# Gated MLP stage on one core: values normalised on ACT behind the next tile's gelu, transposes and last spatial products one output tile later, the last stores on two queues

## The chip, the core and the metric

The kernel runs on one core of a Trainium2 chip. The metric is the device time of one execution in microseconds (us). A core has five engines with an instruction queue each, and each works through its own queue in order: PE (matmul; PEld is its weight load), DVE (vector), ACT (activation), POOL (the general engine) and SP (which here issues DMAs). They meet only through semaphores: an instruction waits until those that write its inputs, or that still read the buffer it will overwrite, have signalled.

## The reference, cut to what matters

Three layers follow one another: attention with a learned position bias, an MLP with a layer norm, and a gated MLP. The change lies in the gated MLP, the last 230 us or so. With x of shape 4 x 576 x 512 and d_ff of 1024:

```python
h = x @ w_in
h = 0.5 * h * (1.0 + np.tanh(c * (h + 0.044715 * h ** 3)))     # gelu
u, v = (h[..., :d_ff // 2], h[..., d_ff // 2:])
mu = np.mean(v, axis=-1, keepdims=True)
var = np.mean((v - mu) ** 2, axis=-1, keepdims=True)
v_n = (v - mu) / np.sqrt(var + 1e-06) * g_ln
v_s = np.einsum('ts,bsd->btd', w_sg, v_n) + b_sg[None, :, None]
gated = u * v_s
return (x + gated @ w_out).astype(np.float32)
```

## The kernel before

Every product runs as three matmul products of split operands (a high and a low part: high by high, high by low, low by high), so each result that feeds a product is split by two instructions: the high part is copied out on ACT (`split_hi`, L110), the low part is the difference, on POOL or DVE (`split_lo`, L113).

The gated MLP is a list of groups, `seq`, worked off by `step`. There are five kinds, for batch element b:

- `g_T` ("transpose"): four PE transposes of a 128-row tile of x into one of two PSUM tiles `pt` (L490), copied out and split into `x2h` (ACT) and `x2l` (DVE).
- `g_v` ("value tile"): 12 matmuls into `psa` (L117), gelu, then layer norm without its gain, then the split into `blk` (or into `vre` and `vro` for the tile that holds the 64 leftover rows of two batch elements).
- `g_u` ("u tile"): 24 matmuls of 288 columns into `psa` (L1210), gelu.
- `g_s` ("spatial product"): 28 matmuls of 288 columns (L1228) with the values as weights, multiplied by u on DVE (L1237, L1238), split.
- `g_o` ("output tile"): 12 matmuls (L117), the residual added on DVE (L1260), stored by DMA.

`psa` has three buffers, so a group's matmuls wait until the group three places before has been read out of PSUM for the last time; for a value or u tile that last read is L1154, the end of its gelu. `pt` has two buffers, so a transpose waits for the `x2l` of the second transpose before it. The SBUF tile `v`, of which there are three, holds a value tile until its low part is taken, and an output tile until it is stored.

The gelu is four instructions in turn: Square on ACT (L1148), L1149 on DVE, Tanh on ACT (L1153), L1154 on DVE. `gelu` returns them as two functions, `first` (Square, L1149) and `second` (Tanh, L1154). For a value tile `second` goes on with the row statistics on DVE (L466, L467). What is left of a group is put off to the next steps: `step` first issues the group's matmuls, then goes through three places (z = 0, 1, 2), issuing in each what earlier groups left for that place and then the group's own function. A value tile leaves for the next step the inverse root of the variance on POOL (`scale`, L470 and L471; L473 and L474 too where the subtraction is folded into a bias) in place 0, the normalisation itself (`apply`, in place, of tile `v`) in place 1 and the copy of the high part in place 2, and for the step after that the low part on POOL in place 0.

`seq` interleaves the groups by `mix`, which takes one of each list in turn. Value tiles come in four batches, 5, 4, 5 and 4 of them, with four u tiles behind the first batch, output tiles of the element before and transposes of the element after mixed behind the second and third, and two output tiles, an `idle` step and the spatial products behind the last. Below, "batch b" means the value tiles of element b and what follows them. Output tiles are stored by SP; the tile j = 4 holds leftover rows of two elements and is stored as two halves.

Of the kernel before, what the change touches and what calls it, by code (L numbers as in the profile page):

```python
# [93 lines left out]
def block_kernel(  # L94
# [6 lines left out]
    act, dve, pool, pe, sp = nc.scalar, nc.vector, nc.gpsimd, nc.tensor, nc.sync  # L101

    def new_pool(name, bufs, stack=None, **kw):
        return (stack or ctx).enter_context(tc.tile_pool(name=name, bufs=bufs, reuse_waits="tile", **kw))
# [4 lines left out]
    def split_hi(o, i, **kw):  # L109
        act.activation(o, i, AF.Copy, **kw)  # L110

    def split_lo(o, i, hi, eng=None):
        (eng or dve).tensor_tensor(out=o, in0=i, in1=hi.bitcast(F32), op=ALU.subtract)  # L113

    def product(ps, terms, start=True, stop=True):
        for j, (w, x) in enumerate(terms):
            pe.matmul(ps, lhsT=w, rhs=x, start=start and j == 0, stop=stop and j == len(terms) - 1)  # L117
# [148 lines left out]
    with ExitStack() as c:  # L266
# [21 lines left out]
        for f in (load_q, load_k):  # L288
# [9 lines left out]
            out=W.rearrange("p (g h) -> p g h", h=8), in0=w8.unsqueeze(1).to_broadcast([128, 4, 8]), in1=ind.unsqueeze(2).to_broadcast([128, 4, 8]), op=ALU.mult,  # L298
# [157 lines left out]
    def block_pair(p):  # L456
        return [p.tile([128, 4, 512], F32R, name="blk") for _ in range(2)]

    def norm_parts(sm, src, eps, dst, eng):

        s6 = sm.tile([128, 6], F32, name="s6")
        mv = sm.tile([128, 2], F32, name="mv")
        rs = sm.tile([128, 2], F32, name="rs")

        def stats():
            dve.bn_stats(out=s6, in_=src)  # L466
            dve.bn_aggr(out=mv, in_=s6)  # L467

        def scale():
            pool.tensor_scalar(out=mv[:, 1:2], in0=mv[:, 1:2], scalar1=eps, scalar2=1.0, op0=ALU.add, op1=ALU.mult)  # L470
            pool.tensor_tensor(out=rs[:, 0:1], in0=mv[:, 1:2], in1=mhalf, op=ALU.pow)  # L471
            if eng is not dve:
                pool.tensor_scalar(out=mv[:, 0:1], in0=mv[:, 0:1], scalar1=-1.0, scalar2=0.0, op0=ALU.mult, op1=ALU.add)  # L473
                pool.tensor_tensor(out=rs[:, 1:2], in0=mv[:, 0:1], in1=rs[:, 0:1], op=ALU.mult)  # L474

        def apply():
            if eng is act:
                act.activation(dst, src, AF.Identity, scale=rs[:, 0:1], bias=rs[:, 1:2])
            elif eng is pool:
                pool.tensor_scalar(out=dst, in0=src, scalar1=rs[:, 0:1], scalar2=rs[:, 1:2], op0=ALU.mult, op1=ALU.add)  # L480
            else:
                dve.tensor_scalar(out=dst, in0=src, scalar1=mv[:, 0:1], scalar2=rs[:, 0:1], op0=ALU.subtract, op1=ALU.mult)  # L482

        return stats, scale, apply
# [37 lines left out]
    def ln_T(blk, j):  # L522
        p = transpose4(xn[blk][j][0])
        th, tl = xT[blk]
        o = slice(128 * j, 128 * j + 128)
        split_hi(th[:, :, o], p)
        split_lo(tl[:, :, o], p, th[:, :, o])
# [112 lines left out]
    with ExitStack() as c:  # L640
        smp = new_pool("asm", 1, c)
        sm = smp.tile([128, 48], F32, name="sm")
# [228 lines left out]
        for u in range(-1, NU):  # L871
            for w in SEQ:
                du, name, *args = w.split()
                v, args = u + int(du), list(map(int, args))
# [54 lines left out]
    def T_groups(b):  # L929
        return [g_T(b, j) for j in ([4] if b % 2 == 0 else []) + [0, 1, 2, 3]]  # L930
# [4 lines left out]
    with ExitStack() as c:  # L935
# [125 lines left out]
        for blk in range(5):  # L1061
# [9 lines left out]
            T = [lambda j=j: ln_T(blk + 1, j) for j in range(len(tiles[blk + 1]))] if blk < 4 else []  # L1071
# [63 lines left out]
    sm = new_pool("qsm", 4)  # L1135
# [7 lines left out]
    def gelu(T, dst, cols):  # L1143


        def first():
            q = T["s"] = tp.tile([128, S], F32, name="sq")[:, :cols[0] * cols[1]].rearrange("p (a b) -> p a b", a=cols[0])
            act.activation(q, T["p"], AF.Square, scale=GELU_SQ)  # L1148
            dve.scalar_tensor_tensor(out=q, in0=q, scalar=GELU_C, in1=T["p"], op0=ALU.add, op1=ALU.mult)  # L1149

        def second():
            q = T["s"]
            act.activation(q, q, AF.Tanh)  # L1153
            dve.scalar_tensor_tensor(out=dst(), in0=q, scalar=1.0, in1=T["p"], op0=ALU.add, op1=ALU.mult)  # L1154

        return first, second

    def g_v(b, j):
        T = {}

        def pe_():
            xh, xl = x2R[b // 2] if j == 4 else [t[:, :, 128 * j:128 * j + 128] for t in x2T[b]]
            T["p"] = psA.tile([128, 2, 512], F32, name="psa")[:, :1]
            product(T["p"][:, 0], [(x[:, k], w[:, k]) for x, w in ((xh, vh), (xh, vl), (xl, vh)) for k in range(4)])
            if j == 0:
                vn[b] = block_pair(wb)
            if j == 4:
                vr[b // 2] = [vp.tile([128, 512], F32R, name="vre"), vp.tile([128, 512], F32R, name="vro")]

        def dst():  # L1170
            T["v"] = tv.tile([128, 512], F32, name="v")
            return T["v"].unsqueeze(1)

        first, second_ = gelu(T, dst, (1, 512))

        def second():
            second_()
            T["n"] = norm_parts(sm, T["v"], 4e-6, T["v"], dve)
            T["n"][0]()

        def parts():

            if j < 4:
                return [(slice(0, 128), vn[b][0][:, j], vn[b][1][:, j])]
            e, o = vr[b // 2]
            return [(slice(0, 64), e[:64], e[64:]), (slice(64, 128), o[64:], o[:64])]

        def post():
            for r, hi, _ in parts():
                split_hi(hi, T["v"][r])  # L1190

        def late_():
            for r, hi, lo in parts():
                split_lo(lo, T["v"][r], hi, pool)

        return pe_, first, second, [(lambda: T["n"][1](), lambda: T["n"][2](), post), (late_, None, None)]

    def g_u(b, m):
# [51 lines left out]
    def g_o(b, j):  # L1250
        T = {}

        def pe_():
            gh, gl = gr[b // 2] if j == 4 else [t[:, :, 128 * j:128 * j + 128] for t in gT[b]]
            T["p"] = psA.tile([128, 2, 512], F32, name="psa")[:, 0]
            product(T["p"], [(x[:, k], w[:, k]) for x, w in ((gh, oh), (gh, ol), (gl, oh)) for k in range(4)])

        def first():
            o = tv.tile([128, 512], F32, name="v")
            dve.tensor_tensor(out=o, in0=T["p"], in1=x_sb[:, 4 * b + j if j < 4 else 16 + b // 2], op=ALU.add)  # L1260
            if j < 4:
                sp.dma_start(out=out[b, 128 * j:128 * j + 128], in_=o)
            else:
                for q in range(2):
                    sp.dma_start(out=out[b - 1 + q, 512:], in_=o[64 * q:64 * q + 64])

        return pe_, first, None, []

# [2 lines left out]
    def step(g):  # L1271
        pe_, first, second, later = g
        now = [q.pop(0) for q in live][::-1]
        pe_()
        for z, own in ((0, first), (1, second), (2, None)):
            for f in now:
                if f[z]:
                    f[z]()
            if own:
                own()  # L1280
        live[:] = [q for q in live if q]
        if later:
            live.append(list(later))

    def idle():
        return (lambda: None), None, None, []

    def v_groups(b):
        return [g_v(b, j) for j in ([4] if b % 2 == 0 else []) + [0, 1, 2, 3]]

    def mix(*lists):

        return [g for n in range(max(map(len, lists))) for x in lists for g in x[n:n + 1]]

    s = {b: [g_s(b, d) for d in range(4)] for b in range(B)}
    u = {b: [g_u(b, d) for d in range(4)] for b in range(B)}
    o = {b: [g_o(b, j) for j in range(4)] + ([g_o(b, 4)] if b % 2 else []) for b in range(B)}
    t = {b: T_groups(b) for b in range(1, B)}
    seq = v_groups(0) + u[0] + mix(s[0][:3], t[1]) + [s[0][3]] + u[1]
    seq += [t[2][0]] + v_groups(1) + mix(o[0], t[2][1:]) + mix(s[1], u[2])  # L1300
    seq += v_groups(2) + mix(o[1], t[3]) + mix(s[2], u[3])
    seq += v_groups(3) + o[2][:2] + [idle()] + s[3] + o[2][2:] + o[3]
    seq += [idle() for _ in range(4)]
    for n, g in enumerate(seq):
        mark(f"gmlp {n}")
        step(g)
# [54 lines left out]
def build(tc, nc, aps, out):  # L1361
    a = {n: (p.bitcast(I32) if n in ("moe_w_ch1", "moe_w_ch2", "moe2_w_in", "moe2_w_out") else p) for n, p in aps.items()}
    with tc.manual_schedule():
        block_kernel(tc, nc, a, out)
# [18 lines left out]
```

## Time and profile before

| | |
|---|---|
| runs | 982.79, 987.43, 988.38 us; median 987.43 us |
| profiled execution | 982.66 us, its span in the trace 980.7 us |
| granted TensorE clock | 0.993 of full speed on average |
| PE, DVE, ACT, POOL busy | 96%, 77%, 50%, 46% of the span |

All rows below are of the one profiled execution; its times count from the start of the span. The end of a matmul is modelled in the trace, so a stretch without PE work is best read from the starts of matmuls. "x12" behind a row means that twelve instructions in a row were merged; "[0.59 <-DVE v L1154]" means that the engine stood idle for 0.59 us before it, until that instruction released it.

### The profile page before, as it was taken

To read this page: it belongs to the slowest core of one execution; us is meant where nothing else is said; L and a number is where in the kernel's file an instruction comes from. 1 tells how busy PE (TensorE), PEld (TensorE's weight loads), DVE (VectorE), ACT (ScalarE), POOL (GpSimd) and SP (SyncE) were. 2 spreads that over 40 slices of the span, in tenths; PEclk is the share of its full clock that TensorE was granted. 3 is DMA by queue.
4 is the path that set the end of the run, shared out by engine and by line. 5 is a ranking of instruction groups with operands and counts; after the bars stand their busy time and mean duration, and the time that the engine had idled before them with its cause. 6 is when DMAs were issued, how large, how long until landed. Compare 5 with 4: busy or idle time off the path is not lost. (4 is left out here: it accounts for less than half of the span.)

```text
span 980.7 us, 16000 instructions
## 1 busy us (share of the span) xinstructions
PE 937.7 (96%) x5729; PEld 813.9 (83%) x5729; DVE 754.9 (77%) x1460; ACT 485.7 (50%) x1090; POOL 450.9 (46%) x556
## 2 busy tenths in 40 slices
PE   7879999999898999999999999999999999998998
PEld 2269998989898878888888888888888897988986
DVE  8989888899887858886769797979765847475462
ACT  8969987989797854322222222323132434242320
POOL 0086997989899744332314334333300423132241
PEclk9999999999999999999999999999999999999999
DMA  7875445436443271113022333332213000001002
GB/s 245 280 265 187 160 153 181 152 124 199 140 143 121 67 257 68 44 31 106 21 99 93 119 95 119 95 118 91 101 65 121 1 2 22 22 1 54 1 23 75
DMA packets 53007, 104.49 MB, mean 107 GB/s; under 512 B 9152, under 2 KB 20160, under 8 KB 52672
## 3 DMA queue, kind: packets, MB, share of 16 engines
q1 hardware_dynamic: 52096, 103.02, 31.3%
q8 instruction: 45, 0.74, 0.3%
q10 hardware_dynamic: 832, 0.46, 0.2%
q14 instruction: 34, 0.28, 0.1%
HBM read 75.08 MB, written 28.38 MB: 105 GB/s over the span
## 5 line engine op out<-in xcount | busy, mean ns | idle before, releaser
L170 POOL TENSOR_TENSOR cvl<-cvl,cvt 128x512 f32<-128x512 f32 x44 | 56.9, 1292 | 206.3 <-DVE cvt L167 186.8
L117 PE MATMUL psh<-blk,w1h 128*128 128x512 f32 (+1 forms) x640 | 151.4, 368 | 0.0
L636 ACT ACTIVATE hh<-psh 128x512 fp32r<-128x512 f32 (+1 forms) x80 | 43.9, 552 | 185.7 <-PE psh L117 177.7
L117 PEld LDWEIGHTS psh<-blk,w1h 128*128 128x128 f32 x640 | 113.5, 188 | 20.7 <-DVE hl L637 0.3
L689 DVE CUSTOM_DVE_ANT_0 ct<-s,bias 128x576 f32<-128x576 f32 x144 | 107.4, 753 | 24.6 <-PE s L683 15.0
L703 ACT ACTIVATE a<-ct,sm 128x576 f32<-128x576 f32 x144 | 112.2, 779 | 3.3 <-POOL v L107 2.3
L1031 DVE TENSOR_TENSOR x_sb<-psy,x_sb 128x512 f32<-128x512 f32 x144 | 97.3, 683 | 9.1 <-PE psy L117 8.6
L709 PE MATMUL pt<-ident,a 128*128 128x128 f32 x576 | 87.1, 279 | 13.8 <-DVE at0l L113 13.8
L637 DVE SCALAR_TENSOR_TENSOR hl<-psh,hh 128x512 fp32r<-128x512 f32 (+1 forms) x80 | 50.5, 633 | 56.0 <-ACT hh L636 55.9
L117 PE MATMUL psy<-w2h,hh 128*128 128x512 f32 x288 | 90.4, 395 | 0.1
L117 PE MATMUL psy<-w2l,hh 128*128 128x512 f32 x288 | 89.0, 390 | 0.0
L117 PE MATMUL psy<-w2h,hl 128*128 128x512 f32 x288 | 88.8, 390 | 0.0
L709 PEld LDWEIGHTS pt<-ident,a 128*128 128x128 f32 x576 | 70.6, 143 | 15.7 <-DVE at0l L113 15.4
L117 PE MATMUL psh<-blk,w1l 128*128 128x512 f32 (+1 forms) x320 | 79.0, 368 | 0.0
L683 PE MATMUL s<-kh,q 128*128 128x288 f32 x320 | 73.5, 320 | 2.7 <-DVE sm L689 0.9
L683 PE MATMUL s<-kl,q 128*128 128x288 f32 x320 | 66.5, 298 | 0.0
L117 PEld LDWEIGHTS psh<-blk,w1l 128*128 128x128 f32 x320 | 56.8, 189 | 10.0
L117 PEld LDWEIGHTS psy<-w2h,hl 128*128 128x128 f32 x288 | 54.1, 188 | 11.5
L117 PEld LDWEIGHTS psy<-w2l,hh 128*128 128x128 f32 x288 | 54.0, 188 | 11.4
L171 POOL TENSOR_TENSOR cvw<-cvl,cvw 128x512 f32<-128x512 f32 x44 | 59.9, 1362 | 3.5
L117 PEld LDWEIGHTS psy<-w2h,hh 128*128 128x128 f32 x288 | 52.4, 188 | 10.5 <-DVE x_sb L1031 0.8
L683 PEld LDWEIGHTS s<-kh,q 128*128 128x128 f32 x320 | 50.0, 194 | 6.0 <-POOL q L113 1.5
(193 smaller groups left out, 2233.1 us busy)
## 6 DMA issues: line engine op xcount, KB each, us to landing
r<-in_moe_w_ch_dram SPq DMA_DIRECT2D x32, 512.0 KB, 4.6
k<-in_k_dram SPq DMA_DIRECT2D x16, 640.0 KB, 5.2
q<-in_q_dram SPq DMA_DIRECT2D x16, 576.0 KB, 4.1
scr<-o SPq DMA_DIRECT2D x24, 295.5 KB, 3.7
v<-in_v_dram SPq DMA_DIRECT2D x16, 320.0 KB, 3.8
bias<-scr SPq DMA_DIRECT2D x8, 576.0 KB, 7.6
bias<-scr SPq DMA_DIRECT2D x8, 512.0 KB, 7.5
wc<-cvw SPq DMA_DIRECT2D x16, 256.0 KB, 2.4
```

The lines of the kernel that those rows point to most:

```text
L117: pe.matmul(ps, lhsT=w, rhs=x, start=start and j == 0, stop=stop and j == len(terms) - 1)
L170: pool.tensor_tensor(out=T["l"], in0=T["l"], in1=T["t"].bitcast(F32), op=ALU.mult)
L171: pool.tensor_tensor(out=T["w"], in0=T["l"], in1=T["w"], op=ALU.add)
L636: act.activation(hh[:, f, :n], ps[:, :n], AF.Relu)
L637: dve.scalar_tensor_tensor(out=hl[:, f, :n], in0=ps[:, :n], scalar=0.0, in1=hh[:, f, :n].bitcast(F32), op0=ALU.max, op1=ALU.subtract)
L683: pe.matmul(s[:, x, :288], lhsT=w, rhs=m[:, 288 * x:288 * x + 288], start=j == 0, stop=j == len(prs) - 1)
L689: dve.tensor_tensor_reduce(out=ct, in0=s[:, :, :288], in1=bias[UNITS[u][0]][:, n].rearrange("p (a b) -> p a b", a=2), scale=-0.125, scalar ...
L703: act.activation(weights(n), ct.rearrange("p a b -> p (a b)"), AF.Exp, scale=-1.0, bias=mt, accum_out=SU[u % 2][:, n:n + 1])
L709: pe.transpose(PA[k % 2][:, j], e[:, 128 * j:128 * j + 128], ident)
L1031: dve.tensor_tensor(out=x_sb[:, t], in0=ps, in1=x_sb[:, t], op=ALU.add)
```

## The change

It has four parts. The normalisation of a value tile (`apply`) is done by ACT (L478) instead of DVE (L482), which makes `scale` issue L473 and L474 too. In `step`, the group's own `second` is issued before what earlier groups left for place 1. In `seq`, one output tile comes first and only then do output tiles and transposes alternate; and behind the last batch of values three output tiles come instead of two and an `idle`, so that one less stands behind the spatial products. The second half of an output tile j = 4 is stored from ACT's queue instead of SP's.

```diff
@@ -1175,7 +1175,7 @@
         def second():
             second_()
-            T["n"] = norm_parts(sm, T["v"], 4e-6, T["v"], dve)
+            T["n"] = norm_parts(sm, T["v"], 4e-6, T["v"], act)
             T["n"][0]()
@@ -1261,8 +1261,8 @@
             if j < 4:
                 sp.dma_start(out=out[b, 128 * j:128 * j + 128], in_=o)
             else:
-                for q in range(2):
-                    sp.dma_start(out=out[b - 1 + q, 512:], in_=o[64 * q:64 * q + 64])
+                for q, e in enumerate((sp, act)):
+                    e.dma_start(out=out[b - 1 + q, 512:], in_=o[64 * q:64 * q + 64])
@@ -1273,10 +1273,12 @@
         now = [q.pop(0) for q in live][::-1]
         pe_()
         for z, own in ((0, first), (1, second), (2, None)):
+            if own and z == 1:
+                own()
             for f in now:
                 if f[z]:
                     f[z]()
-            if own:
+            if own and z == 0:
                 own()
@@ -1297,9 +1299,9 @@
-    seq += [t[2][0]] + v_groups(1) + mix(o[0], t[2][1:]) + mix(s[1], u[2])
-    seq += v_groups(2) + mix(o[1], t[3]) + mix(s[2], u[3])
-    seq += v_groups(3) + o[2][:2] + [idle()] + s[3] + o[2][2:] + o[3]
+    seq += [t[2][0]] + v_groups(1) + o[0][:1] + mix(o[0][1:], t[2][1:]) + mix(s[1], u[2])
+    seq += v_groups(2) + o[1][:1] + mix(o[1][1:], t[3]) + mix(s[2], u[3])
+    seq += v_groups(3) + o[2][:3] + s[3] + o[2][3:] + o[3]
```

What this does to DVE's queue, in batch 2, between the gelu of one value tile and the gelu of the next. Before (the number behind a name tells one buffer from another):

```order
L466 BN_STATS s6_9228<-v_9226 128x6
L467 BN_AGGR mv_9229<-s6_9228 128x2
L1149 SCALAR_TENSOR_TENSOR sq_9252<-sq_9252,psa_9235 128x512
L482 TENSOR_SCALAR v_9226<-v_9226,mv_9229,rs_9230 128x512
L1154 SCALAR_TENSOR_TENSOR v_9257<-sq_9252,psa_9235 128x512
```

The same place on DVE with the change:

```order
L466 BN_STATS s6_9247<-v_9245 128x6
L467 BN_AGGR mv_9248<-s6_9247 128x2
L1149 SCALAR_TENSOR_TENSOR sq_9274<-sq_9274,psa_9255 128x512
L1154 SCALAR_TENSOR_TENSOR v_9278<-sq_9274,psa_9255 128x512
L466 BN_STATS s6_9280<-v_9278 128x6
```

L482 has stood between a tile's L1149 and its L1154 and is gone. ACT's queue over the same step, which holds the gelu of one tile (Square L1148, Tanh L1153) and the copy of the tile before it, before the change:

```order
L1148 ACTIVATE sq_9252<-psa_9235 128x512
L1153 ACTIVATE sq_9252<-sq_9252 128x512
L110 ACTIVATE blk_9217<-v_9226 128x512
L1148 ACTIVATE sq_9281<-psa_9265 128x512
L1153 ACTIVATE sq_9281<-sq_9281 128x512
```

And with it:

```order
L1148 ACTIVATE sq_9274<-psa_9255 128x512
L1153 ACTIVATE sq_9274<-sq_9274 128x512
L478 ACTIVATE v_9245<-v_9245,rs_9249 128x512
L110 ACTIVATE blk_9235<-v_9245 128x512
L1148 ACTIVATE sq_9305<-psa_9287 128x512
```

L478 of the tile before now stands between a tile's Tanh and the copy. On PE, the end of the output tiles and transposes of batch 2, where the spatial products (L1228) begin, as a piece of the difference:

```order
 L490 MATMUL pt_74<-ident,x_sb 128x128 x4
-L117 MATMUL psa<-blk 128x512 x12
-L490 MATMUL pt_73<-ident,x_sb 128x128 x4
 L117 MATMUL psa<-blk,grh 128x512 x8
 L117 MATMUL psa<-blk,grl 128x512 x4
+L490 MATMUL pt_73<-ident,x_sb 128x128 x4
 L1228 MATMUL psa<-sgh,vre 128x288 x2
```

One output tile has moved ahead of the first transpose (so it is missing here), and the last transpose (L490) has moved behind the last output tile (`grh`, `grl`).

## Rows read from the trace of the kernel before

**Rows 1.** Timeline, DVE and POOL, batch 2: start, duration, engine, line, operation.

```profile
870.26 0.55 DVE L482 TENSOR_SCALAR v<-v,mv,rs 128x512 f32<-128x512 f32 x1 [0.38 <-POOL rs L471]
...
876.89 0.55 POOL L471 TENSOR_TENSOR rs<-mv,mhalf 128x1 f32<-128x1 f32 x1
...
877.41 1.28 POOL L113 TENSOR_TENSOR blk<-v,blk 128x512 fp32r<-128x512 f32 x1
877.48 1.50 DVE L482 TENSOR_SCALAR v<-v,mv,rs 128x512 f32<-128x512 f32 x1 [0.45 <-POOL rs L471]
...
881.46 1.51 DVE L482 TENSOR_SCALAR v<-v,mv,rs 128x512 f32<-128x512 f32 x1 [0.38 <-POOL rs L471]
```

**Rows 2.** Timeline, batch 2, from the first transpose to the first spatial product.

```profile
879.01 0.60 PE L490 MATMUL pt<-ident,x_sb 128*128 128x128 f32 x4
...
887.01 0.63 ACT L110 ACTIVATE blk<-v 128x512 fp32r<-128x512 f32 x1 [3.37 <-DVE v L482]
...
888.15 0.69 DVE L113 TENSOR_TENSOR x2l<-pt,x2h 128x512 fp32r<-128x512 f32 x1 [1.18 <-ACT x2h L110]
...
888.90 0.66 PE L490 MATMUL pt<-ident,x_sb 128*128 128x128 f32 x4 [2.19 <-DVE x2l L113]
...
892.17 0.60 PE L490 MATMUL pt<-ident,x_sb 128*128 128x128 f32 x4
...
895.36 0.42 PE L1228 MATMUL psa<-sgh,vre 128*128 128x288 f32 x2
```

**Rows 3.** Timeline, PE, batch 0: first value tile, first u tile, first spatial product.

```profile
750.89 1.98 PE L117 MATMUL psa<-blk,rh 128*128 128x512 f32 x8
...
764.49 2.28 PE L1210 MATMUL psa<-x2h,blk 128*128 128x288 f32 x16
...
779.26 0.42 PE L1228 MATMUL psa<-sgh,vre 128*128 128x288 f32 x2
```

**Rows 4.** Chain of work that ended last: four u tiles of the next element.

```profile
796.07 12.80 PE psa L1210 x96
```

**Rows 5.** Timeline, PE, batch 1: a transpose, and the first spatial product.

```profile
822.78 0.60 PE L490 MATMUL pt<-ident,x_sb 128*128 128x128 f32 x4
...
834.86 0.51 PE L1228 MATMUL psa<-sgh,vro 128*128 128x288 f32 x2
```

**Rows 6.** Timeline, PE, batch 3: first matmuls of three spatial products.

```profile
939.96 0.50 PE L1228 MATMUL psa<-sgh,vro 128*128 128x288 f32 x2 [0.38 <-DVE v L1154]
...
945.64 0.43 PE L1228 MATMUL psa<-sgh,vro 128*128 128x288 f32 x2
...
949.36 0.43 PE L1228 MATMUL psa<-sgh,vro 128*128 128x288 f32 x2
```

**Rows 7.** Timeline, the gelu of the first value tile, with ACT and DVE free.

```profile
753.87 0.60 ACT L1148 ACTIVATE sq<-psa 128x512 f32<-128x512 f32 x1 [9.03 <-PE psa L117]
754.50 0.69 DVE L1149 SCALAR_TENSOR_TENSOR sq<-sq,psa 128x512 f32<-128x512 f32 x1 [2.72 <-ACT sq L1148]
...
755.22 0.63 ACT L1153 ACTIVATE sq<-sq 128x512 f32<-128x512 f32 x1 [0.76 <-DVE sq L1149]
...
755.89 0.69 DVE L1154 SCALAR_TENSOR_TENSOR v<-sq,psa 128x512 f32<-128x512 f32 x1 [0.70 <-ACT sq L1153]
```

**Rows 8.** Instructions by line, in the earlier MLP: ns least/median/most, first and last start.

```profile
L478 ACT ACTIVATE t<-x_sb,rs x10: 805/816/819, 358.5 to 388.4; 128x512 f32<-128x512 f32 x10
...
L474 POOL TENSOR_TENSOR rs<-mv,rs x18: 189/190/193, 318.4 to 388.2; 128x1 f32<-128x1 f32 x18
```

**Rows 9.** Timeline, the end: last residual, then the two half stores.

```profile
976.08 0.69 DVE L1260 TENSOR_TENSOR v<-psa,x_sb 128x512 f32<-128x512 f32 x1 [2.03 <-PE psa L117]
976.80 1.11 SPq L1265 DMA_DIRECT2D out_dram<-v  x2
```

**Rows 10.** DMA issues: queue, count, KB each, median us from issue to landing.

```profile
out_dram<-v SPq DMA_DIRECT2D x4, 128.0 KB, 2.3
...
xs<-x ACTq DMA_DIRECT2D x1, 256.0 KB, 5.2
```

## The prediction

> **What bounds the kernel now.** I read the page first: PE is busy 96% of the span, and the chain of work that ended last is mostly PE, so a gain must come from stretches where PE stands still. Then I read the timeline of the gated MLP for the starts of matmuls, and compared each stretch with what the same matmuls take where nothing holds them. Only four stretches fall short, each behind a batch of value tiles.
>
> Batch 2: the last transpose starts at 892.17 and what follows its output tile at 895.36, so a transpose and an output tile take 3.19 [rows 2]. The first transpose starts at 879.01; four such pairs would bring PE to the spatial products at 891.77. They start at 895.36: 3.59 lost.
> Batch 0: from the first u tile to the first spatial product 14.77 pass [rows 3]; four undisturbed u tiles take 12.80 [rows 4]: 1.97 lost.
> Batch 1: from a transpose at 822.78 to the spatial product at 834.86 are 12.08 [rows 5], for three pairs of 3.19 and one lone transpose (0.60 at most): 1.91 lost.
> Batch 3: 0.38 idle ahead of the first spatial product, which then takes 5.68 to the start of the next, where an undisturbed one takes 3.72 [rows 6]: 2.34 lost.
> Together 9.81 us. These are starts of matmuls, so stretched ends don't enter.
>
> What PE waits for is DVE. From one L482 to the next 3.98 pass [rows 1], while PE makes a value tile in 2.72 (five between 750.89 and 764.49, [rows 3]). Of the 3.98, L482 itself is 1.50. In [rows 1] it takes 0.55 where POOL is not at a low part, and 1.50 where POOL's L113 (1.28) started 0.07 ahead of it. So DVE falls behind by 1.26 a tile, the gelu's last read of `psa` (L1154) comes late, and later the copies out of `pt` do too: `x2l` of the transpose of 879.01 is done at 888.84, and the third transpose starts at 888.90 [rows 2].
>
> The Trainium skill, "SBUF — State Buffer", section "Who interferes with whom", says why: a DVE tensor_scalar in a two-port mode and a GpSimd instruction hold a shared port pair each for its whole length, and ACT never waits for it. The trace agrees with the first half by the 0.55 and the 1.50; no row shows L478 beside POOL's L113.
>
> **The change, part by part.**
>
> *Normalisation on ACT.* 18 of L482 leave DVE; of its 3.98 a tile 2.48 are left, under PE's 2.72. ACT gains 18 of L478 at 0.82, measured in the earlier MLP on the same shape [rows 8]. POOL gains L473 and L474 per tile, some 0.19 each [rows 8], beside 0.55 for L471 and 1.28 for L113 [rows 1]: still under PE's 2.72.
>
> The new thing to watch is ACT, since a tile's gelu crosses to DVE and back inside its queue. From Square to Tanh are 1.35 with DVE free [rows 7]; then Tanh 0.63, L478 0.82, the copy 0.63 [rows 2]: 3.43 a tile at whole lengths. That is under DVE's 3.98 and over PE's 2.72, so PE's lead shrinks within a batch and is won back behind it. The lead: the first tile's L1154 ends 5.69 after its matmuls began (750.89 to 756.58, [rows 3, 7]), and its buffer is needed three tiles on, at 8.16: 2.47 to spare. The second tile loses perhaps 0.2, having no L478 ahead of it. The third of a five-tile batch has L478 and two copies (`vre`, `vro`, 0.63 each) ahead: 4.06 against 2.72, leaving about 0.9. Fourth: 0.71 less, 0.2. Fifth: -0.5 against value tiles, but what PE does by then is longer (u tiles of 3.20, or 3.19 with a transpose), so about 0. Four-tile batches have no second copy and stay positive. I keep 0 to 0.5 of waiting in each of the two long batches, and take 0.3 each: -0.6.
>
> *`second` ahead of what earlier tiles left.* It puts L478 behind the next tile's Tanh. If L478 stood ahead, the Tanh would wait for POOL's `rs`. As written it costs nothing that the 3.43 does not hold. Queued behind an L478 that waits are the copy and the next Square; the 3.43 counts all three.
>
> *Output tile ahead of the transposes.* Same matmuls, another order. In batch 2 the third transpose then comes at 879.01 + 2.72 + 2 x 3.19 = 888.11. It needs the first one's `x2l`. That was done at 888.84; ahead of it on DVE two L482 of 1.50 go, and for the last tile L478 (0.82) and two small POOL operations (0.38) come in: 888.84 - 3.00 + 1.20 = 887.04, 1.07 ahead. What becomes later is the last transpose, now directly ahead of the spatial products; the u tile that needs its copy is one spatial product of 3.72 away [rows 6], as it was.
>
> *Three output tiles, no idle step, in batch 3.* The 2.72 of the third tile stand over the 1.96 that the first spatial product lost waiting for the last high and low parts, even if these come no earlier. The cover is taken from the end: between the last spatial product and the output tiles of element 3 stands one output tile of 2.72 instead of 5.44. The high part is ready after two DVE operations and a copy, by the nearest rows 0.69 + 0.69 + 0.63 and some latency, 2.3 (an estimate), and the low part 1.28 later, 3.6; it is first read by the ninth of twelve matmuls, at 2.72 + 1.8 = 4.5. So this costs nothing, with 0.9 to spare; without any cover it would cost 3.6.
>
> *Two store queues.* The two half stores at the end take SP 1.11 [rows 9]. With one on ACT the second is issued some 0.55 sooner. Below: nothing, or a loss, since the nearest store on ACT's queue landed after 5.2 against 2.3 on SP [rows 10], 2.9 worse less 0.55. That one had twice the bytes, so I take -0.5 from the end. The same store in batch 2 stands in ACT's queue ahead of the last `x2h`, and waits there for L1260; half of 1.11 beside the 3.72 of the spatial product that separates it from its reader: nothing.
>
> Sum: 9.81 + 0.5 - 0.6 = 9.7 us. Against the profiled execution, 982.66 - 9.7 = 973.0, a ratio of 0.9901. That execution lies with the lowest of the three runs; the median is 987.43. Applied to it: **977.7 us**.
>
> **Rivals.**
>
> *ACT becomes what PE waits for.* Each tile's copy reads what L478 wrote, so it may wait for L478's end and a signal; one or two such gaps of 0.3 would make 3.7 or more of the 3.43. Halfway between 3.43 and DVE's 3.98 I count half the gain: 4.9 less, 977.8, or 982.5 on the median's scale. For it: the leads above are near 0 at the end of the two long batches. Against it: two batches have a lead over 0.5 throughout, and batch 3 and the transposes gain by order alone. The Trainium skill, "ScalarE: Activation LUTs", section "Rules for kernel authors", speaks for it: add and multiply belong on VectorE, not on ScalarE. By the rows that would be 0.82 against 0.55, a loss of 0.27 a tile; but only where DVE's 0.55 is to be had, and fourteen of the eighteen take some 1.50.
>
> *Slower: L478 is stretched beside POOL's low part as L482 was.* By 0.95 (1.50 less 0.55) it would be 1.77 and ACT's step 4.38, 0.40 over DVE's 3.98; over the 14 tiles that have one ahead of them in their batch 5.6 us, less 0.5 at the end: 987.8, or 992.6 on the median's scale. It turns from gain to loss where L478 reaches 1.37. Against it: [rows 8] has L478 within 805 to 819 ns over ten.
>
> *It does not do what it says.* If L1154 waited for the variance rather than for its place behind L482, moving L482 would shift the wait to ACT. L482 stood idle 0.38 to 0.45 for `rs` [rows 1]; the rest is its own length. Then the order alone stays: some 2.3 of batch 3, and I call it 985 on the median's scale.
>
> **How the numbers follow.** Full gain 0.80; ACT-paced 0.12; stretched 0.04; order alone 0.04. 0.5%, some 4.9 us, is about what a measurement of this kernel tells from no change. Full gain is faster; half of the ACT-paced case too: 0.86 faster. The other half and order alone: 0.10 same; 0.04 slower. For the range: the full gain by itself, 8.0 to 10.5, is 977 to 979.5 on the median's scale; the three runs differ by 5.6, and the profiled execution with that gain would be 972 to 975, so the low end is 971. The high end takes in the ACT-paced case: 983.
>
> **What would show it.** Right: no L482; L1154 of successive value tiles some 3.2 to 3.4 apart instead of 4.0; PE from 879.01's counterpart to the spatial products without a wait of over 0.5; the first spatial product of batch 3 in 3.72; L478 at 0.82 beside POOL's L113; the last store on ACT's queue landing with the one on SP. Wrong: waits of u, output or spatial matmuls on L1154 of over 1 us in total; L478 over 1 us; waits ahead of the first output tile of element 3; a span that falls by less than PE's lost time does.

## The result, and the profile after

The changed kernel takes 975.51 us (median of 6 runs, 969.68 to 977.37) against 985.73 for the kernel before (6 runs, 982.79 to 988.38): a ratio of 0.9886, 95% interval 0.9858 to 0.9914. The forecast was 977.7 us, 971 to 983, faster. Its profiled execution took 969.68 us, against 982.66.

First the page: the span, the busy time of each engine, and the chain that ended last by engine.

```profile
span 967.9 us, 16019 instructions
...
PE 932.9 (96%) x5729; PEld 810.9 (84%) x5729; DVE 733.9 (76%) x1442; ACT 499.5 (52%) x1108; POOL 458.9 (47%) x592
...
PE 28%; DVE 0%; issue 0%
```

DVE has 18 instructions fewer, ACT 18 more, POOL 36 more (L473 and L474). The chain is now PE's, with DVE and "issue" under half a per cent of the span; before, DVE held 5% of it:

```profile
PE 20%; DVE 5%; POOL 1%; ACT 1%; issue 1%; POOLq 0%; ACTq 0%; DVEq 0%
```

Next, windows over the gated MLP: length, then busy time of PE, PEld, DVE, ACT and POOL with instruction counts, the granted clock, the DMA share and GB/s.

```profile
750.00:840.00 90.00, 90.00 (x577) 83.77 (x576) 50.58 (x78) 43.73 (x74) 31.99 (x60) 1.00 0.11 43
840.00:900.00 60.00, 60.00 (x369) 54.73 (x368) 30.18 (x46) 25.43 (x44) 21.64 (x38) 1.00 0.07 23
900.00:963.00 63.00, 63.00 (x367) 56.95 (x366) 28.29 (x42) 18.41 (x34) 19.04 (x33) 1.00 0.09 34
```

PE is busy in all 213 of 213 us, and the trace lists no wait of PE in this stage. Before, the largest were these (who waited for whom: us in total, times, longest):

```profile
PE pt L490 <- DVE x2l L113: 4.1, 2, 2.2
PE psa L1210 <- DVE u L1154: 0.7, 1, 0.7
PE psa L117 <- DVE v L1154: 0.6, 1, 0.6
PE psa L1210 <- DVE v L1154: 0.6, 1, 0.6
```

The timeline of batch 2 shows what took the place of [rows 1, 2] (start, duration, engine, line; the idle time before it in brackets).

```profile
870.83 0.63 ACT L1153 ACTIVATE sq<-sq 128x512 f32<-128x512 f32 x1 [0.75 <-DVE sq L1149]
...
871.27 1.29 POOL L113 TENSOR_TENSOR blk<-v,blk 128x512 fp32r<-128x512 f32 x1
871.37 0.80 ACT L478 ACTIVATE v<-v,rs 128x512 f32<-128x512 f32 x1
871.57 0.69 DVE L1154 SCALAR_TENSOR_TENSOR v<-sq,psa 128x512 f32<-128x512 f32 x1 [0.77 <-ACT sq L1153]
872.20 0.63 ACT L110 ACTIVATE blk<-v 128x512 fp32r<-128x512 f32 x1
872.74 0.58 ACT L1148 ACTIVATE sq<-psa 128x512 f32<-128x512 f32 x1
...
874.07 0.63 ACT L1153 ACTIVATE sq<-sq 128x512 f32<-128x512 f32 x1 [0.75 <-DVE sq L1149]
...
874.81 0.69 DVE L1154 SCALAR_TENSOR_TENSOR v<-sq,psa 128x512 f32<-128x512 f32 x1 [0.77 <-ACT sq L1153]
...
879.08 0.69 DVE L1260 TENSOR_TENSOR v<-psa,x_sb 128x512 f32<-128x512 f32 x1 [2.05 <-POOL blk L113]
...
879.83 0.69 DVE L113 TENSOR_TENSOR x2l<-pt,x2h 128x512 fp32r<-128x512 f32 x1
...
881.67 0.60 PE L490 MATMUL pt<-ident,x_sb 128*128 128x128 f32 x4
```

Three things are to be seen. L478 takes 0.80 although POOL's L113 started 0.10 ahead of it; L482 took 1.50 in that place [rows 1]. ACT now paces the values: from one Tanh (L1153) to the next are 3.24, and DVE's L1154 waits for the Tanh each time. (From one L1154 to the next it is 3.24 to 3.51, but 2.9 for the second tile of a batch and 4.3 for the third of a long one.) And the low part of the batch's first transpose is done at 880.52, 1.15 ahead of the third transpose (881.67), which has no wait; in [rows 2] that transpose waited 2.19.

Batch 3 answers to [rows 6]: PE, and POOL's last low part.

```profile
932.12 0.42 PE L1228 MATMUL psa<-sgh,vro 128*128 128x288 f32 x2
...
935.83 0.43 PE L1228 MATMUL psa<-sgh,vro 128*128 128x288 f32 x2
...
949.65 1.30 POOL L113 TENSOR_TENSOR x2l<-sq,x2h 128x512 fp32r<-128x512 f32 x1 [2.23 <-ACT x2h L110]
949.78 1.98 PE L117 MATMUL psa<-blk,x2h 128*128 128x512 f32 x8
951.59 1.07 PE L117 MATMUL psa<-blk,x2l 128*128 128x512 f32 x4
```

The first spatial product takes 3.71 instead of 5.68. The last low part is done at 950.95, 0.64 ahead of the matmul that reads it. The end answers to [rows 9], with the landing times of the half stores (count, KB each, us) from the DMA issues.

```profile
963.58 0.69 DVE L1260 TENSOR_TENSOR v<-psa,x_sb 128x512 f32<-128x512 f32 x1 [2.03 <-PE psa L117]
...
964.29 0.49 SPq L1265 DMA_DIRECT2D out_dram<-v  x1
964.30 0.50 ACTq L1265 DMA_DIRECT2D out_dram<-v  x1
```

```profile
out_dram<-v SPq DMA_DIRECT2D x2, 128.0 KB, 2.5
out_dram<-v ACTq DMA_DIRECT2D x2, 128.0 KB, 2.8
```

From the last L1260 to the end of the span are 4.32, before 4.62 (976.08 to 980.7): 0.30 less. The end of the span is printed to 0.1 us, so this number and the totals below hold to about 0.05.

**Where the time went, by stretch.** The table holds starts of matmuls in each profiled execution: b0 is from the first value tile's matmul to the first spatial product, b1 and b2 likewise; b3 is from its first value tile to the last L1260; the end is from there to the end of the span. The stretches between batches add up to 85.3 to 85.5 in every kernel and are left out. "Gated MLP" is the whole, from the first value matmul to the end of the span. The rows below the second are the experiments.

| kernel | b0 | b1 | b2 | b3 | end | gated MLP | against before |
|---|---|---|---|---|---|---|---|
| before | 28.37 | 25.80 | 32.70 | 53.00 | 4.62 | 229.81 | |
| the change | 26.53 | 23.64 | 29.22 | 50.53 | 4.32 | 219.70 | -10.11 |
| the change, run again | 26.51 | 23.63 | 29.19 | 50.52 | 4.36 | 219.71 | -10.10 |
| norm on ACT and step edit | 26.50 | 24.23 | 31.00 | 51.48 | 4.62 | 223.21 | -6.60 |
| new order alone | 28.37 | 24.04 | 30.62 | 51.15 | 4.62 | 224.21 | -5.60 |
| the change without step edit | 31.35 | 26.02 | 33.22 | 53.37 | 4.34 | 233.72 | +3.91 |
| step edit alone | 32.52 | 27.27 | 37.10 | 54.54 | 4.59 | 241.34 | +11.53 |
| low parts on DVE | 27.31 | 24.36 | 31.61 | 50.80 | 4.68 | 224.07 | -5.74 |
| low parts on DVE, new order | 27.32 | 23.64 | 29.96 | 50.53 | 4.63 | 221.48 | -8.33 |
| the change, ACT longer | 30.36 | 23.89 | 31.31 | 51.22 | 4.29 | 226.55 | -3.26 |
| the change, full tile last | 26.52 | 23.64 | 29.21 | 50.52 | 3.89 | 219.25 | -10.56 |

In its two executions the changed kernel repeats within 0.04 us in every column, far better than whole runs do. So mechanisms are read from this table. The ratios confirm its direction, not its sizes: in all seven comparisons with several runs of the kernel tried, its median stands lower against before than the table says, by 0.1 to 5.6 us. The new order alone and the last section come back to this. The span fell by 12.8, of which 10.11 are this stage; the other 2.69 passed ahead of it (the first value matmul starts at 748.20 instead of 750.89), where the program is the same, and the last section shows the part of the clock in them.

### The profile page after: what moved, and what is told of

Read it like the earlier page. It is cut to its first block, busy times and chain, and to the rows that moved or that the text cites. A ratio compares the mean times of both kernels' runs of the same rounds, so it can differ in the third digit from the quotient of the medians.

```text
span 967.9 us, 16019 instructions
## 1 busy us (share of the span) xinstructions
PE 932.9 (96%) x5729; PEld 810.9 (84%) x5729; DVE 733.9 (76%) x1442; ACT 499.5 (52%) x1108; POOL 458.9 (47%) x592
## 5 line engine op out<-in xcount | busy, mean ns | idle before, releaser
L117 PEld LDWEIGHTS psh<-blk,w1l 128*128 128x128 f32 x320 | 56.8, 188 | 10.1
```

## The experiments

The theory: PE waits for DVE, whose turn per value tile is long because L482 is stretched beside POOL's low part; moving the normalisation to ACT behind the next Tanh shortens the turn, and the later transposes give the rest. The rivals: ACT becomes what PE waits for; the gain is not the normalisation's, but the order's.

**The change again**, for the ratio and for whether the 2.69 us belong to it.

> The change as it is, beside the three runs that take it apart. In the trace after, the gated MLP from its first matmul to the end of the span is 10.1 us shorter than before, and another 2.7 us were gained ahead of it, where the program is the same. If only the former is the change's, the ratio over five rounds is 0.9897 (10.1 of 982.7); if the latter belongs to it too, 0.987. Within the trace: 1.8, 2.2, 3.5 and 2.5 us from batches 0, 1, 2 and 3, and 0.3 from the end.

973.82 us (4 runs, 972.26 to 975.86), ratio 0.9881 (0.9865 to 0.9897); the gated MLP again 219.71. The ratio doesn't settle the question, since its interval holds 0.987 and, at its edge, 0.9897. The trace does: the first value matmul started at 752.69 this time, later than before's. So the change's own part is 10.1 us, or 0.9898 of 986.27, the median of before beside it; what lies ahead of the gated MLP moves between executions of one kernel.

**Normalisation on ACT with the step edit, old order and stores.**

```diff
-            T["n"] = norm_parts(sm, T["v"], 4e-6, T["v"], dve)
+            T["n"] = norm_parts(sm, T["v"], 4e-6, T["v"], act)
...
+            if own and z == 1:
+                own()
             for f in now:
...
-            if own:
+            if own and z == 0:
```

> Normalisation on ACT with the group's own second part first; groups in the order of before, both half stores on SP. Theory (DVE's queue made PE late; both the normalisation and the order of groups work on that same lateness): batch 0 gains its whole 1.8; in batches 1 and 2 the third transpose still comes before the copy of the first is out, so these gain about 1.6 and 1.7 of 2.2 and 3.5; batch 3 about 1.5 of 2.5. 6.6 us, ratio about 0.993. Rival (the order of groups is what counts): under 3 us, ratio 0.997 or more. Rival (all is DVE's load): 9 us or more, ratio 0.991 or less.

978.9 us, ratio 0.9932 (0.992 to 0.9944); 6.60 us in the trace. Batch 0, where the order is the same as before, is healed wholly (26.50). What is left are waits of the transposes and of a spatial product, as the waits of PE say (columns as above).

```profile
PE pt L490 <- DVE x2l L113: 2.0, 2, 1.6
PE psa L1228 <- POOL blk L113: 0.6, 1, 0.6
```

**The new order alone.**

```diff
-    seq += [t[2][0]] + v_groups(1) + mix(o[0], t[2][1:]) + mix(s[1], u[2])
-    seq += v_groups(2) + mix(o[1], t[3]) + mix(s[2], u[3])
-    seq += v_groups(3) + o[2][:2] + [idle()] + s[3] + o[2][2:] + o[3]
+    seq += [t[2][0]] + v_groups(1) + o[0][:1] + mix(o[0][1:], t[2][1:]) + mix(s[1], u[2])
+    seq += v_groups(2) + o[1][:1] + mix(o[1][1:], t[3]) + mix(s[2], u[3])
+    seq += v_groups(3) + o[2][:3] + s[3] + o[2][3:] + o[3]
```

> Only the new order of groups; normalisation on DVE as before, both half stores on SP. Theory: batch 0, which has no changed order, keeps its loss of 2.0; batch 1 gains about 1.9, batch 2 about 2.2 (output tiles now wait 0.6 and 0.9 for L1154), batch 3 about 2.0. 6.1 us, ratio about 0.994: so the two parts overlap, 6.6 and 6.1 for 9.8 together. The prediction on record put the order alone at 2.3 us, ratio 0.9977; if that holds, the parts add rather than overlap.

5.60 us in the trace: 1.76, 2.08 and 1.85 in batches 1 to 3, nothing in batch 0. The waits of the transposes are gone; those on L1154 remain, and two output tiles of batch 2 now have one too. It is the mirror image of the kernel above (same columns):

```profile
PE psa L117 <- DVE v L1154: 1.5, 3, 0.6
PE psa L1210 <- DVE u L1154: 0.6, 1, 0.6
PE psa L1210 <- DVE v L1154: 0.6, 1, 0.6
```

The runs gave 975.12 us (6 runs, 972.96 to 982.52), ratio 0.9902 (0.9872 to 0.9932), where 5.60 us would be 0.9943. Three of its six executions had a granted clock of 0.995 or 0.996 and took 972.96 to 973.77, three had 0.990 to 0.992 and took 976.47 to 982.52; none of the eleven of before beside it was over 0.993. At a like clock the size fits: before, in a later series, took 978.43 to 979.77 at 0.995 or 0.996, which is 4.7 to 6.8 above the three. The trace is the better measure here.

**The change without the step edit**: L478 stands ahead of the next tile's Tanh.

```diff
-            if own and z == 1:
-                own()
             for f in now:
                 if f[z]:
                     f[z]()
-            if own and z == 0:
+            if own:
                 own()
```

> The change without its edit of the step: the tile before is normalised ahead of the group's Tanh. Theory: Tanh then waits for POOL's scale, and the way Tanh, L1154, statistics, POOL, L478, next Tanh lies in series: about 0.66 + 0.72 + 0.73 + 0.3 + 1.3 + 0.7 = 4.4 us from one L1154 to the next instead of 3.25, longer than the 3.98 of before. Gain falls from 10 to about 1.5 us, ratio about 0.9985. Rival (the edit of the step only tidies up and ACT has room): spacing stays near 3.3, ratio 0.990.

989.51 us, ratio 1.0038 (1.0026 to 1.005): slower than before, where the expectation had it slightly faster; 3.91 us in the trace. The spacing of L1154 is 4.38 to 4.53, near what was expected; what it costs PE was set too low. Batch 2, ACT and the operations it waits for:

```profile
879.22 0.18 DVE L467 BATCH_NORM_AGGREGATE mv<-s 128x2 f32<-128x6 f32 x1
...
880.57 0.19 POOL L474 TENSOR_TENSOR rs<-mv,rs 128x1 f32<-128x1 f32 x1
880.80 0.82 ACT L478 ACTIVATE v<-v,rs 128x512 f32<-128x512 f32 x1 [1.26 <-POOL rs L474]
...
881.52 0.61 ACT L1153 ACTIVATE sq<-sq 128x512 f32<-128x512 f32 x1
...
882.16 0.69 DVE L1154 SCALAR_TENSOR_TENSOR v<-sq,psa 128x512 f32<-128x512 f32 x1 [1.91 <-ACT sq L1153]
```

ACT stands idle 1.26 for POOL's four small operations, the Tanh stands behind L478, and DVE stands idle 1.91 for the Tanh.

**The step edit alone**: the normalisation stays on DVE, behind the tile's own L1154. It separates the two edits made together in the kernel with the normalisation on ACT.

```diff
+            if own and z == 1:
+                own()
             for f in now:
...
-            if own:
+            if own and z == 0:
```

> Before, with one edit: a tile's second stage (Tanh, L1154, the statistics) stands ahead of what earlier tiles left, and the normalisation stays on DVE (L482). It separates the two edits that the kernel with the norm on ACT made together. Theory (the step edit only pays because ACT does the normalisation): in before, L482 fills the time in which DVE waits for the Tanh; put behind L1154 it leaves DVE idle some 0.7 for each Tanh and still takes 1.50 beside POOL, so L1154 to L1154 becomes 0.7 + 0.68 + 0.70 + 0.18 + 0.66 + 1.50 = 4.4 in place of 4.0; by the kernel with the other order of norm and Tanh (4.46, gated MLP 233.7 from first value matmul to the end of the span) the gated MLP takes 231 to 234 against 229.8 of before. Rival (the order of the steps is what gained, not the engine): 3.2 to 3.5 a tile, gated MLP 223 to 225.

One run of 994.96 us against 984.47 beside it; 11.53 us slower in the trace, worse than the theory asked, and the rival is out. Some 1.65 of the 11.53 are one fall of the clock in this execution: behind a wait of 2.48 the granted clock fell to 0.50 from 898.2 to 901.7, and the transpose and output tile there took 4.85 (898.13 to 902.98) instead of 3.2. The other ten traces have no fall in the gated MLP ahead of the last matmul. The spacing is mostly 4.70, and not for the reason given: fifteen of the eighteen L482 are not stretched here (0.51 to 0.54; the three that run beside POOL's L113 take 1.58 to 1.59). The rows form a ring.

```profile
767.64 0.58 ACT L1148 ACTIVATE sq<-psa 128x512 f32<-128x512 f32 x1
...
768.26 0.69 DVE L1149 SCALAR_TENSOR_TENSOR sq<-sq,psa 128x512 f32<-128x512 f32 x1 [1.18 <-ACT sq L1148]
768.98 0.63 ACT L1153 ACTIVATE sq<-sq 128x512 f32<-128x512 f32 x1 [0.75 <-DVE sq L1149]
769.71 0.69 DVE L1154 SCALAR_TENSOR_TENSOR v<-sq,psa 128x512 f32<-128x512 f32 x1 [0.77 <-ACT sq L1153]
...
771.26 0.52 DVE L482 TENSOR_SCALAR v<-v,mv,rs 128x512 f32<-128x512 f32 x1
771.81 0.63 ACT L110 ACTIVATE blk<-v 128x512 fp32r<-128x512 f32 x1 [2.20 <-DVE v L482]
772.35 0.58 ACT L1148 ACTIVATE sq<-psa 128x512 f32<-128x512 f32 x1
```

Square, L1149, Tanh, L1154, statistics, L482, the copy on ACT, and only then the next Square: 767.64 to 772.35 is 4.71. The copy waits 2.20 for L482 and holds up the Square queued behind it. In the change the same order costs nothing, since L478 is on the copy's own engine and the copy starts 0.03 after it (872.17 to 872.20).

**The low parts of the values on DVE**, all else as before. This takes POOL's L113 away from beside L482, and puts 0.69 on DVE in its place.

```diff
-                split_lo(lo, T["v"][r], hi, pool)
+                split_lo(lo, T["v"][r], hi)
```

> The kernel before, with the low parts of the values taken on DVE instead of POOL. It is for the length of L482 alone. Theory (L482 is long because POOL's L113 holds what both use): with no L113 of the values on POOL all 18 of L482 take about 0.55. Rival (its length comes from reading a tile that was just written, or from waiting for POOL's result): fourteen of them keep 1.50. DVE's step would be 3.98 - 1.50 + 0.55 + 0.70 = 3.73 under the theory, some 4.7 under the rival.

One run of 977.55 us beside a median of 985.95; 5.74 us in the trace. L482 takes 540 to 625 ns in all eighteen (mean 1296 before), and the spacing falls from 4.0 to 3.50 although DVE has one operation more. That shows the stretch beside POOL's low part to be the cause of DVE's long turn. What it is that the two share, no run here takes apart. The 3.73 that was expected kept DVE's idle time for POOL's `rs`, which went from 6.1 us ahead of sixteen L482 to 1.5 ahead of four. Before, then with the low parts on DVE (count, ns least/median/most, first and last start):

```profile
L482 DVE TENSOR_SCALAR v<-v,mv,rs x18: 545/1508/1531, 758.5 to 941.7; 128x512 f32<-128x512 f32 x18
L482 DVE TENSOR_SCALAR v<-v,mv,rs x18: 540/547/625, 758.6 to 937.6; 128x512 f32<-128x512 f32 x18
```

**The same with the new order** (the edits of the two kernels above, and no other).

> Before, with two edits: the new order of the output tiles and transposes, and the low parts of the value tiles on DVE, so that L482 has no POOL low part beside it; normalisation stays on DVE and the step edit is not made. Theory (PE waits for DVE, and DVE's step is long by the stretched L482; any way to shorten it serves): L1154 to L1154 3.50 and batch 0 27.3, as with the low parts alone; batches 1 to 3 lose what is left of both, some 0.6 together, so 221 to 222 from the first value matmul to the end of the span, against 219.7 of the change, 224.1 and 224.2 of the two edits alone. Rival (the two gains are of the same wait, and do not add): 223.5 to 224.

221.48 in the trace, as the theory had it (221 to 222): 8.33 of the change's 10.11 without ACT taking anything over. Its one run of 980.21 us started the gated MLP at 756.32, the latest of all. Batches 1 and 3 lose nothing; two waits on L1154 are left, in batches 0 and 2:

```profile
PE psa L117 <- DVE v L1154: 0.4, 1, 0.4
PE psa L1210 <- DVE u L1154: 0.3, 1, 0.3
```

**The change with a longer turn on ACT**: ahead of L478 a second pass over the tile, whose output nothing reads.

```diff
+    spare = new_pool("qspare", 1).tile([128, 512], F32, name="spare")
...
+        def twice():
+            act.activation(spare, T["v"], AF.Identity, scale=0.5, bias=mhalf)
+            T["n"][2]()
...
-        return pe_, first, second, [(lambda: T["n"][1](), lambda: T["n"][2](), post), (late_, None, None)]
+        return pe_, first, second, [(lambda: T["n"][1](), twice, post), (late_, None, None)]
```

> The change, with a second ACT instruction like L478 (same shape, into a tile that nothing reads) ahead of each L478. Theory (ACT paces the value batches, at 3.25 a tile, and PE's lead just covers it): the spacing of L1154 goes up by the 0.70 that ACT needs from the start of one L478 to the next instruction, to about 3.95, as on DVE before; batch 0 loses about 2 again, batch 2 about 1.3, batch 3 about 0.4, batch 1 nothing. Gain 6.3 us, ratio about 0.9935. Rival (ACT has room; half busy in the windows): spacing stays, ratio 0.990.

982.01 us (10 runs), ratio 0.9967 (0.9941 to 0.9994); 3.26 us faster in the trace instead of 10.1, and about half of the 6.3 that were expected. The longer turn makes the spacing 4.05 to 4.13 instead of 3.24 to 3.31, and PE waits on L1154 again. The spacing was forecast within 0.2; what it costs PE was set too low, above all in batch 0, which loses 3.83 and not 2: its third tile comes 4.85 after the second. So ACT does pace the values, and the rival "ACT becomes what PE waits for" is a question of 0.8 us a tile.

**The change with the leftover tile first among the last outputs**, so that the last store is one of a full tile on SP.

```diff
-    seq += v_groups(3) + o[2][:3] + s[3] + o[2][3:] + o[3]
+    seq += v_groups(3) + o[2][:3] + s[3] + o[2][3:] + o[3][4:] + o[3][:4]
```

> The change, with the output tile of leftover rows (two half stores) first instead of last among the output tiles of element 3, so that a full tile with one store of 256 KB ends the program. Theory (half stores land 2.4 to 2.6 after their issue, full ones after 2.0): from the start of the last residual add to the end of the span 4.32 shrinks to about 3.8. Rival: the end is the same, since a last store of any size takes what it takes. In the ratio neither can be told from 0.990.

973.07 us (4 runs), ratio 0.9891 (0.9841 to 0.9941); the end takes 3.89 instead of 4.32 to 4.36. It is the shortest stage of all, 219.25, by an amount that whole runs don't resolve. The Trainium skill, "DMA: Bandwidth & Descriptors", section "Rules for kernel authors", advises one transfer over all partitions instead of two over halves; the 0.43 is in line with it, though here the two half stores remain and only stand earlier.

## Why the prediction was right

**What bounds the stage.** The losses read from [rows 2 to 6] were 1.97, 1.91, 3.59 and 2.34, in sum 9.81. The stretches became shorter by 1.84, 2.16, 3.48 and 2.47, in sum 9.95. Taking what PE's starts lack against undisturbed matmuls as the whole prize was right, batch by batch to 0.25. Two of the four were read a little short: the lone transpose of batch 1 takes 0.36 (834.50 to 834.86) and not 0.60, and the 0.38 in batch 3 is idle time behind a modelled end, where the starts lack 0.54. That makes 2.15 and 2.50, beside the 2.16 and 2.47 won.

**PE waits for a DVE stretched by POOL.** Shown by the low parts on DVE: L482 at 0.55, spacing 3.50, 5.74 us. The rule that the prediction quotes from the Trainium skill, "SBUF — State Buffer", section "Who interferes with whom", agrees in its second half too: L478 took 808 ns on average over all eighteen, at 0.80 beside L113. In its first half it agrees in kind: an L482 that began only where L113 ended would make a row of 1.28 - 0.07 + 0.55 = 1.76, and the row is 1.50. The rival that ends slower needed an L478 of 1.37.

**Waits that stay behind an ACT-paced batch, 0.6 off the gain.** Mis-sized; nothing stayed. The turn on ACT is 3.24, not 3.43: the estimate added whole lengths, but start to start the Tanh is 0.54 and the copy 0.54 (870.83, 871.37; 872.20, 872.74), each 0.09 under its 0.63. The feared gap between L478 and the copy is 0.03. The third tile was later than thought, 4.28 after the second instead of 4.06, and the leads still held.

**Output tile ahead of the transposes.** `x2l` 1.07 ahead was forecast, 1.15 measured. The path that the working took (the last L478 and the copies behind it) does end there; a second one, which it left out, ends at the same moment: on DVE the residual add (L1260) queued ahead of that `x2l` stood idle 2.05 for POOL's low part of an earlier value tile, whose buffer `v` it writes, and was done at 879.77, `x2l` starting at 879.83. For the last low part 0.9 to spare was forecast, 0.64 measured.

**Two store queues, 0.5 off the end.** 0.30; the store on ACT's queue landed in 2.8 against 2.5.

**The step edit.** "It costs nothing that the 3.43 does not hold" was right, and too modest about its weight. Without it the change is 3.91 us slower than before; alone it is 11.53 slower, of which the fall of the clock is some 1.65. Two edits that are each a loss in the company tried make 6.60 together.

**The step that failed** lies in a rival: "the order alone gives some 2.3 of batch 3". It gives 5.60. The working counted the transposes' gain only together with the shorter DVE turn; yet by its own numbers (`x2l` at 888.84, the third transpose moved to 888.11) a wait of 2.19 would have shrunk to 0.73 with the order alone. In the run it went altogether, though `x2l` came no earlier (26.2 after the batch's first matmul in both kernels): PE came later, held by L1154 ahead of two output tiles, 0.55 and 0.56. So the two halves of the change overlap: 5.60 and 6.60 and 0.30 for the stores are 12.5, and together they give 10.1. Most of the overlap is in batches 1 and 3, where 1.76 + 1.57 and 1.85 + 1.52 stand over 2.16 and 2.47. By the stage's 5.60, the 985 that the rival named would have been some 3 us too high.

The median came out 2.2 us under the forecast. 0.5 of it is the sum (the medians differ by 10.2, for 9.7); 1.7 is that the three runs of before shown then had a median of 987.43 and the six have 985.73. In the sum two sizes that were wrong partly cancel, 0.6 of waits that never came and 0.2 of the stores that did not come off; that the medians differ by almost the stage's 10.11 is in part luck, since both sets of six mix executions of unlike clock.

## What to carry to other kernels

Where PE waits in several places behind one slow turn of another engine, price the stretch by what its matmuls' starts lack: that is the prize, and it does not tell which edit wins it, since shortening the turn and moving the reader later heal some of the same waits. Before moving an operation to another engine, write out the ring from one tile's first operation to the next tile's, with every queue that it passes: the same order of two steps was needed with the operation on ACT and ruinous with it on DVE. And look for an operation with two very different lengths at one line: what runs beside the long ones is worth moving in a run of its own. Here that edit of one word gave 5.74, where moving the operation and reordering the steps gave 6.60.

## What the hardware showed that was not expected

The program ahead of the gated MLP is the same in all eleven traces, yet their first value matmul starts anywhere from 748.20 to 756.32. Part of it is TensorE's clock. In the kernel before it stood in these windows (columns as above; the third last is the granted clock) around a wait of PE that ends at 149.79 (2.35 long):

```profile
148.00:150.00 2.00, 0.20 (x2) 0.21 (x3) 2.00 (x4) 0.41 (x1) 1.92 (x3) 1.00 0.00 0
150.00:152.00 2.00, 2.00 (x13) 1.95 (x12) 1.97 (x6) 1.35 (x3) 1.85 (x2) 0.70 0.00 0
152.00:154.00 2.00, 2.00 (x10) 1.99 (x10) 1.02 (x4) 1.06 (x4) 1.89 (x2) 0.50 0.00 0
```

PE had all but stood still, and the clock then fell to 0.50, the lower of its two levels (1.2 of 2.4 GHz). The same place in the changed kernel, where the wait was 2.21:

```profile
148.00:150.00 2.00, 0.00 (x0) 0.00 (x1) 2.00 (x3) 0.74 (x3) 1.92 (x3) 1.00 0.00 0
150.00:152.00 2.00, 2.00 (x16) 2.00 (x17) 2.00 (x5) 1.31 (x3) 1.91 (x2) 1.00 0.00 0
152.00:154.00 2.00, 2.00 (x19) 1.76 (x18) 1.96 (x9) 1.98 (x7) 1.83 (x3) 1.00 0.00 0
```

PE stood still as well, and the clock stayed. The 10 us around a fall show a clock of 0.83, so a fall costs some 1.7 us of full-speed work. Before the gated MLP the profile of before has four (at 60, 150, 250 and 310), that of the change two (at 60 and 300): 3.4 us less, where the stage began 2.69 earlier. Whole runs sort the same way: in one series of thirteen before took 978.43 to 979.77 in its three executions at a mean clock of 0.995 or 0.996 and 983.35 to 989.61 in the ten below, and the change 969.68 and 970.28 against 975.25 to 977.37. What decides between the two stays open; no experiment here varied it. The length of the wait alone does not: in the kernel with the step edit alone PE waited 2.46 ahead of 837.7 and kept its clock, and 2.48 ahead of 898.1 and lost it, and over the eleven traces one of 2.17 was followed by a fall (the new order alone, at 150) and one of 3.01 was not (the longer turn on ACT, at 258). Whether the kernels with the change meet fewer falls than before other than by chance is not shown either.
